# Attention's weighted values summed by accumulating DMAs in DRAM, and two more unused matmuls in the head

## The chip, the core and the metric

The kernel runs on one core of one Trainium2 chip. The metric is the device time of one execution in microseconds (us). The engines are TensorE (PE, matmul; PEld is its weight load), VectorE (DVE), ScalarE (ACT), GpSimd (POOL) and SyncE (SP, which here only issues DMAs).

## The reference

The input x is 2048 x 640, float32. It is normalised; a local dilated attention and a gated bilinear network work on the normalised rows, and the result joins both:

```python
xn = _layernorm(x)
qkv = xn @ wqkv                       # 32 heads of 20
idx = pos[:, None] - (arange(8) * 2)  # 8 places, every second row back
logits = einsum("bhsd,bhswd->bhsw", q, k[idx]) * scale   # masked where idx < 0
o = einsum("bhsw,bhswd->bhsd", softmax(logits), v[idx])
s = o @ wo
h = (xn @ w_gate) * (xn @ w_up)       # 640 -> 1536
g = silu(h @ w_down)
return x + s * g
```

## The kernel before

The 2048 rows lie as 16 tiles of 128; a tile holds rows a fixed distance apart, so that the eight places of a row's window lie in the same partition or in the one before it. Matmuls run on high and low halves of each float32 operand in three passes (`mm3`, line 87: high x high, one low, the other low), which a split on ScalarE (line 79, high) and a subtraction, mostly on GpSimd (line 80, low), prepare.

The program is written in one order, engine by engine, and each engine works through its own queue in that order. Its stages:

1. Head: loads, three unused products of the identity (line 147), normalisation and transposes, the first qkv and the first gate and up matmuls.
2. Attention stage, about 110 to 550 us. The heads lie in six groups (5, 5, 5, 5, 6, 6), each group in two halves of eight tiles: twelve units. `unit(u)` computes q, k and v of a unit (`qkv`, 8 x 15 matmuls); between units stand three or four pieces of `gate_up`, each for one f of 12 (128 columns of the network) and one of four chunks of 512 rows: 15 matmuls for the gate (PSUM tile g), 15 for up (u). Their product h goes to DRAM (`h_scr`).
3. The attention of a unit is a generator, `attention(u)`. `advance(budget)` steps it between the matmuls: each yield names about its own VectorE time, and the budget is about the matmuls' time. So the order in which VectorE's work is written follows the credit. Of the eight places two are done at a time (`PAIRS`): four products of q and k with their sums, the softmax, then four products of weights and values (line 279), three additions of pairs (line 287), one of the pair's halves (line 290), and a store into `o_scr` by SP (line 292).
4. The last f (f1): behind its piece 1 the attention is drained, the output weights wo are split (two of five behind each of the first two pieces, one behind the third), and tile 0 of o is loaded. Before its piece 3 stand the load of wd, the transposes of tile 0, and the loads of tiles 1 to 7 of o (`load_o`, line 384).
5. Output projection (16 tiles), then the product with w_down (in seven products for each pair of tiles), gating and the output.

SP issues all DMAs and does it in order: a DMA that waits for an engine holds those behind it. A finished piece multiplies u and g on VectorE while a generator runs (line 333), and with ScalarE and GpSimd otherwise (lines 335, 336).

Tiles with one tag share buffers in rotation: `t` (x tiles, attention's products, o tiles, h tiles) has two.

Of the kernel before, what the change touches and what calls it, by code (L numbers as in the profile page):

```python
# [11 lines left out]
F32 = mybir.dt.float32  # L12
F32R = mybir.dt.float32r
AF = mybir.ActivationFunctionType
ALU = mybir.AluOpType
# [16 lines left out]
GROUPS = [5, 5, 5, 5, 6, 6]  # L32
GOFF = [sum(GROUPS[:g]) * DH for g in range(len(GROUPS))]
# [4 lines left out]
PAIRS = range(0, W, 2)  # L38
# [9 lines left out]
def kernel(  # L48
# [9 lines left out]
    nc = tc.nc  # L58
# [5 lines left out]
    dr = ctx.enter_context(tc.tile_pool(name="dr", bufs=1, space=DRAM))  # L64
# [12 lines left out]
    def split(eng, raw, hi, lo):  # L77

        nc.scalar.activation(hi, raw, AF.Copy)  # L79
        eng.tensor_sub(lo, raw, hi.bitcast(F32))  # L80
# [20 lines left out]
    def split_wq(g, eng, ks=(0, KD)):  # L101
        c3 = 3 * GROUPS[g] * DH
        if g not in wq:
            wq[g] = st([P, KD, c3], "wqh", 1, F32R), st([P, KD, c3], "wql", 1, F32R)
        for k0, k1, t in wq_raw[g]:
            if ks[0] <= k0 < ks[1]:
                split(eng, t, wq[g][0][:, k0:k1], wq[g][1][:, k0:k1])

    wf_raw, wf = {}, {}
# [18 lines left out]
        for i in range(n):  # L128
            xt[s + i] = t[:, i, :]

    xa, xb = st([P, 3, D], "t", 2), st([P, 3, D], "t", 2)
    load_x(0, 1, xa[:, 0:1], (0, HALF, D))
    load_x(1, 1, xa[:, 1:2])
    load_wq(0, ((0, 1, 2, 3), (3, 4, 5)))
# [8 lines left out]
    load_x(15, 1, xb[:, 2:3])  # L143
    ident = st([P, P], "ident", 1)
    make_identity(nc, ident)
    for _ in range(3):
        nc.tensor.matmul(pt([P, 3, P], "q", 4), ident, ident.unsqueeze(1).to_broadcast([P, 3, P]), start=True,
                         stop=True)
    eps_t = st([P, 1], "eps", 1)
    nc.vector.memset(eps_t, EPS)  # L150

    o_scr = [dr.tile([2, P, NE, GROUPS[g] * DH], F32, name=f"o_scr{g}") for g in range(len(GROUPS))]
    h_scr = dr.tile([NT, P, KF, P], F32, name="h_scr")
    s_scr = dr.tile([NT, P, D], F32, name="s_scr")

# [43 lines left out]
    def trans(s):  # L199
        transposed(xt[s], *xT_tile(s))  # L200
# [34 lines left out]
    def attention(u):  # L235
        g, r = UN[u]
        nh = GROUPS[g]
        c = nh * DH
        q, kv = q_t[u], kv_t[u]
        pair, one, small = [(n + 155) / 950 for n in (2 * NE * c, NE * c, NE * nh * W)]  # L240
        lg = st([P, NE * nh, W], "lg", 2)
        e = st([P, NE * nh, W], "e", 1)
        yield 1.0

        def places(a, j):

            y = kv[:, a, j:j + NE, :].rearrange("p i c -> p (i c)")
            return bass.AP(y.tensor, y.offset, [y.ap[0], [c, 2], y.ap[1]])

        def pair_tile():  # L250
            return st([P, 2, NE * c], "t", 2)

        def heads(y):
            return y.rearrange("p a (n d) -> p a n d", d=DH)

        for j in PAIRS:
            t = pair_tile()
            nc.vector.tensor_mul(t, q.rearrange("p i c -> p (i c)").unsqueeze(1).to_broadcast([P, 2, NE * c]),  # L258
                                 places(0, j))
            yield pair  # L260
            nc.vector.tensor_reduce(out=lg[:, :, j:j + 2].rearrange("p n a -> p a n"), in_=heads(t),  # L261
                                    op=ALU.add, axis=AX.X)
            yield pair
        m0 = lg[0:1].rearrange("p (i h) w -> p i h w", h=nh)
        nc.vector.tensor_add(m0, m0, mask.unsqueeze(2).to_broadcast([1, NE, nh, W]))
        sm = st([P, 2, NE * nh], "sm", 2)
        nc.vector.tensor_reduce(out=sm[:, 0, :], in_=lg, op=ALU.max, axis=AX.X)
        nc.vector.tensor_sub(lg, lg, sm[:, 0, :].unsqueeze(2).to_broadcast([P, NE * nh, W]))
        yield 3 * small
        nc.scalar.activation(e, lg, AF.Exp, scale=SCALE)  # L270
        yield small
        nc.vector.tensor_reduce(out=sm[:, 0, :], in_=e, op=ALU.add, axis=AX.X)
        nc.vector.reciprocal(sm[:, 1, :], sm[:, 0, :])
        nc.vector.tensor_mul(e, e, sm[:, 1, :].unsqueeze(2).to_broadcast([P, NE * nh, W]))
        yield 3 * small

        def weighted(j, t):
            pw = e[:, :, j:j + 2].rearrange("p n a -> p a n").unsqueeze(3).to_broadcast([P, 2, NE * nh, DH])
            nc.vector.tensor_mul(heads(t), pw, heads(places(1, j)))  # L279

        acc, t = pair_tile(), pair_tile()
        weighted(PAIRS[0], acc)
        yield pair
        for j in PAIRS[1:]:
            weighted(j, t)
            yield pair
            nc.vector.tensor_add(acc, acc, t)  # L287
            yield pair
        o = st([P, NE, c], "o", 1)
        nc.vector.tensor_add(o.rearrange("p i c -> p (i c)"), acc[:, 0, :], acc[:, 1, :])  # L290
        yield one
        nc.sync.dma_start(o_scr[g][r], o)

    running = []

    def advance(budget):
        credit[0] += budget
        while running and credit[0] > 0:
            try:
                credit[0] -= next(running[0][1])  # L300
            except StopIteration:
                running.pop(0)
        if not running:
            credit[0] = 0
# [75 lines left out]
    def load_o(s, n, t):  # L380

        for g in range(len(GROUPS)):
            c = GROUPS[g] * DH
            nc.sync.dma_start(t[:, :, GOFF[g]:GOFF[g] + c], o_scr[g][s // NE, :, s % NE:s % NE + n, :])
        for i in range(n):
            o_t[s + i] = t[:, i]

    def trans_o(s):
        if s == NT - 2:
            oT[s] = st([P, KD, P], "hs", 2, F32R), st([P, KD, P], "hs", 2, F32R)  # L390
        else:
            tag, n = ("kv", 2) if s == 0 else ("wf", 4) if s < NT - 2 else ("t", 2)
            y = st([P, 2, KD, P], tag, n, F32R)
            oT[s] = y[:, 0], y[:, 1]
        transposed(o_t.pop(s), *oT[s])
# [55 lines left out]
    def load_h(n):  # L451

        a, b = 2 * n, 2 * n + 1
        if n % 2:
            ta, tb = st([P, KF, P], "t", 2), st([P, KF, P], "t", 2)
            nc.sync.dma_start(ta, h_scr[a])
            nc.sync.dma_start(tb, h_scr[b])
            h_raw[n] = {"A11": ta[:, :KH], "A12": ta[:, KH:], "A21": tb[:, :KH], "A22": tb[:, KH:]}
        else:
            h_raw[n] = {}  # L460
            for name, s, k, tag, m in (("A11", a, 0, "wraw", 3), ("A21", b, 0, "wraw", 3),
                                       ("A22", b, KH, "wraw", 3), ("A12", a, KH, "o", 1)):
                h_raw[n][name] = st([P, KH, P], tag, m)
                nc.sync.dma_start(h_raw[n][name], h_scr[s][:, k:k + KH])
# [92 lines left out]
    mv1 = moments(1, 1)  # L557
    split_wq(0, nc.gpsimd, (0, 3))
    trans(0)
    split_wq(0, nc.gpsimd, (3, KD))  # L560
    load_x(13, 1, xa[:, 0:1])
    norm(1, 1, mv1)
# [88 lines left out]
    for ch in range(NCH):  # L651
        gate_up(f0, ch)
        if ch == 0:
# [3 lines left out]
            t = load_wo((4,))  # L657
    for ch in range(NCH):
        if ch == 3:
            load_wd(0)  # L660
            trans_o(0)
            load_o(1, 1, st([P, 1, D], "hs", 2))
            load_o(2, 3, st([P, 3, D], "t", 2))
            load_o(5, 3, st([P, 3, D], "t", 2))
        gate_up(f1, ch)
        if ch < 3:
            for k in ((0, 1), (2, 3), (4,))[ch]:
                split_wo(k)
        if ch == 1:
            drain(len(UN) - 2)  # L670
            load_o(0, 1, t[:, 1:2])
        if ch == 2:
            advance(1e9)

    load_wd(1)
    o_next = {3: (8, 3), 6: (11, 3), 9: (14, 2)}
    n_prod = 7 * NT // 2
    for s in range(NT):
        k, part = divmod(s - 1, 2)
        if s == 1:  # L680
            begin_wd()
        if s + 1 < NT:
            trans_o(s + 1)
        if s in o_next:
            load_o(*o_next[s], st([P, o_next[s][1], D], "t", 2))
# [12 lines left out]
    load_sx(0)  # L698
    load_sx(1)
    load_h(1)  # L700
    AHEAD = 4
    sum_h(1)
# [4 lines left out]
    for m in range(n_prod):  # L707
        n, j = divmod(m, 7)
# [52 lines left out]
```

## Time and profile before

| | |
|---|---|
| median of 3 runs | 804.54 us (803.0 to 804.66) |
| profiled execution | 803.25 us, span 801.5 us |
| granted TensorE clock, mean | 0.998 |
| PE busy | 791.7 us |
| VectorE busy | 635.2 us |
| ScalarE busy | 236.7 us |
| GpSimd busy | 137.7 us |
| moved by DMA | 90.07 MB, 34.7% of 16 engines' span on SP's queue |

The span runs from the first to the last instruction; some 1.8 us of the execution's time lie around it. Busy times overlap between engines. The chain of the page follows the work that ended last back to the start: what stands there sets the time, what does not is hidden. A row of a timeline or of the groups gives, after the arrow in brackets, what ended the idle time before it.

### The profile page before, as it was taken

How to read it: one execution, taken by the hardware profiler on the slowest of the kernel's cores; microseconds unless marked ns; L12 is line 12 of the kernel's file. 1: busy time of each engine (PE TensorE's matmuls, PEld its weight loads, DVE VectorE, ACT ScalarE, POOL GpSimd, SP SyncE). 2: the span in 40 equal slices, each digit the busy share in tenths (PEclk: the TensorE clock that was granted, in tenths of full speed). 3: DMA queues.
4: the chain of work that ended last, by engine and by line, in shares of the span. 5: the costliest groups of instructions: out<-in, count | busy, mean ns of one | idle time of the engine just before them, and what ended most of it. 6: DMA issues, size and time to landing. Idle time of an engine off the chain costs nothing.

```text
span 801.5 us, 11434 instructions
## 1 busy us (share of the span) xinstructions
PE 791.7 (99%) x4564; PEld 721.5 (90%) x4564; DVE 635.2 (79%) x638; ACT 236.7 (30%) x560; POOL 137.7 (17%) x109
## 2 busy tenths in 40 slices
PE   8999999999999999999999999999999999999997
PEld 6889898898898898898989889888899999999997
DVE  7676899999999979997999999990144457878775
ACT  4323212121112111211121112102355554444442
POOL 5201210122012100500231001104266500000000
PEclk9999999999999999999999999999999999999999
DMA  9122012141122221313141222422867464565523
GB/s 318 63 80 89 28 61 79 51 121 48 49 88 86 87 70 60 116 39 97 49 137 42 68 72 78 129 61 75 214 191 206 139 251 136 201 224 185 178 99 132
DMA packets 68413, 90.07 MB, mean 112 GB/s; under 512 B 16952, under 2 KB 48776, under 8 KB 68360
## 3 DMA queue, kind: packets, MB, share of 16 engines
q1 hardware_dynamic: 68360, 89.34, 34.7%
q8 instruction: 36, 0.59, 0.3%
q14 instruction: 17, 0.14, 0.1%
HBM read 51.90 MB, written 28.31 MB: 100 GB/s over the span
## 4 chain that ended last, share of the span: by engine, by line
PE 96%; DMA 1%; POOL 1%; issue 1%; ACT 0%; DVE 0%; SPq 0%; POOLq 0%
PE q L87 35%; PE g L87 20%; PE u L87 20%; PE q L526 10%; PE u L526 5%; PE g L526 3%; PE q L195 2%; DMA wraw<-in_wqkv 1%; DMA hs<-o_scr 0%; POOL wf L80 0%; POOL wql L80 0%; ACT xc L196 0%; DVE q L512 0%; POOL hs L336 0%; SPq L127 0%
## 5 line engine op out<-in xcount | busy, mean ns | idle before, releaser
L87 PE MATMUL g<-xc,wf 128*128 128x512 f32 (+1 forms) x735 | 176.3, 391 | 0.1
L87 PE MATMUL u<-xc,wf 128*128 128x512 f32 (+1 forms) x735 | 176.1, 390 | 0.0
L87 PEld LDWEIGHTS u<-xc,wf 128*128 128x128 f32 x735 | 135.6, 187 | 32.2
L87 PE MATMUL q<-wqh,xc 128*128 128x300 f32 (+1 forms) x960 | 161.8, 311 | 2.1 <-ACT xc L196 1.6
L87 PEld LDWEIGHTS g<-xc,wf 128*128 128x128 f32 x735 | 135.2, 188 | 31.2 <-POOL wf L80 0.3
L87 PEld LDWEIGHTS q<-wqh,xc 128*128 128x128 f32 x960 | 146.8, 189 | 4.2 <-ACT xc L196 2.1
L258 DVE TENSOR_TENSOR t<-q,kv 128x1600 f32<-128x1600 f32 (+1 forms) x48 | 101.7, 2119 | 9.1 <-DMA kv<-kv 9.1
L279 DVE TENSOR_TENSOR t<-e,kv 128x1600 f32<-128x1600 f32 (+1 forms) x48 | 97.6, 2053 | 1.1
L261 DVE TENSOR_REDUCE lg<-t 128x80 f32<-128x1600 f32 (+1 forms) x48 | 92.6, 1930 | 1.2
L322 ACT ACTIVATE gs<-g 128x512 f32<-128x512 f32 x48 | 28.8, 599 | 207.5 <-PE g L87 198.8
L80 POOL TENSOR_TENSOR wf<-wraw,wf 128x256 fp32r<-128x256 f32 (+2 forms) x22 | 44.8, 2053 | 249.1 <-ACT wf L79 249.1
L87 PE MATMUL q<-wql,xc 128*128 128x300 f32 (+1 forms) x480 | 87.0, 311 | 0.2 <-POOL wql L80 0.2
L287 DVE TENSOR_TENSOR t<-t,t 128x1600 f32<-128x1600 f32 (+1 forms) x36 | 78.0, 2166 | 1.1
L226 ACT ACTIVATE kv<-q 128x200 f32<-128x200 f32 (+1 forms) x96 | 33.4, 348 | 145.9 <-PE q L87 145.9
L87 PEld LDWEIGHTS q<-wql,xc 128*128 128x128 f32 x480 | 74.8, 189 | 0.6 <-POOL wql L80 0.5
L526 PE MATMUL q<-xc,wf 128*128 128x320 f32 x432 | 67.3, 309 | 0.0
L526 PEld LDWEIGHTS q<-xc,wf 128*128 128x128 f32 x432 | 64.3, 188 | 0.0
L80 POOL TENSOR_TENSOR wql<-wraw,wqh 128x300 fp32r<-128x300 f32 (+4 forms) x15 | 33.4, 2254 | 147.8 <-ACT wqh L79 147.8
L197 DVE TENSOR_TENSOR wf<-q,wf 128x512 fp32r<-128x512 f32 (+1 forms) x26 | 11.5, 486 | 41.7 <-ACT wf L196 41.7
L87 PE MATMUL q<-wf,wf 128*128 128x320 f32 x156 | 36.8, 317 | 0.0
L197 DVE TENSOR_TENSOR xc<-q,xc 128x512 fp32r<-128x512 f32 (+1 forms) x32 | 13.9, 484 | 20.7 <-ACT xc L196 20.7
L333 DVE TENSOR_TENSOR hs<-u,gs 128x512 f32<-128x512 f32 x39 | 26.6, 683 | 0.8 <-issue 0.8
(144 smaller groups left out, 900.9 us busy)
## 6 DMA issues: line engine op xcount, KB each, us to landing
h_scr<-hs SPq DMA_DIRECT2D x48, 256.0 KB, 2.3
wraw<-in_wgu SPq DMA_DIRECT2D x12, 640.0 KB, 4.5
t<-h_scr SPq DMA_DIRECT2D x8, 768.0 KB, 7.4
s_scr<-gs SPq DMA_DIRECT2D x16, 320.0 KB, 2.3
hs<-s_scr SPq DMA_DIRECT2D x16, 320.0 KB, 3.7
gs<-in_x SPq DMA_DIRECT2D x16, 320.0 KB, 4.2
out<-q SPq DMA_DIRECT2D x15, 320.0 KB, 2.4
wraw<-h_scr SPq DMA_DIRECT2D x12, 384.0 KB, 6.1
```

Of the source, the lines that this page charges most:

```text
L80: eng.tensor_sub(lo, raw, hi.bitcast(F32))
L87: nc.tensor.matmul(acc, a, b, start=first and n == 0, stop=last and n == len(runs) - 1)
L195: nc.tensor.transpose(p[:, k - k0, :], src[:, k * P:(k + 1) * P], ident)
L197: nc.vector.tensor_sub(lo[:, k0:k1, :], p, hi[:, k0:k1, :].bitcast(F32))
L226: nc.scalar.activation(kv_t[u][:, :, W - 1 + i, :], p[:, c:].rearrange("p (a c) -> p a c", a=2), AF.Copy)
L258: nc.vector.tensor_mul(t, q.rearrange("p i c -> p (i c)").unsqueeze(1).to_broadcast([P, 2, NE * c]), places(0, j))
L261: nc.vector.tensor_reduce(out=lg[:, :, j:j + 2].rearrange("p n a -> p a n"), in_=heads(t), op=ALU.add, axis=AX.X)
L279: nc.vector.tensor_mul(heads(t), pw, heads(places(1, j)))
L287: nc.vector.tensor_add(acc, acc, t)
L322: nc.scalar.activation(gs, pp[0], AF.Copy)
L333: nc.vector.tensor_mul(hs, pp[1], gs)
L526: nc.tensor.matmul(p, y[:, i, k], wd_t[name][k][:, l], start=new and r == 0, stop=r == len(runs) - 1, skip_group_check=True)
```

## The change

- The additions of attention's products (lines 287, 290) go. Each of a unit's four products gets a tile of its own. SP stores the first two into two accumulators in DRAM, `o_scr[g][r][0]` and `[1]`; GpSimd issues the third and fourth as DMAs that add to them.
- Two more accumulating DMAs on GpSimd's queue finish a unit: the second accumulator is added to the first, then the first's second half to its first half. `merge()` issues one of them; they wait in a list. It is called in the next unit's generator, behind the third pair of the logits and ahead of the weighted values, and in loops behind pieces 1 and 2 of the last f, which empty the list.
- The yields for the removed additions go too, so a generator ends with less credit.
- `t` has four buffers instead of two, and the program reserves 2048 bytes for GpSimd's DMA descriptors.
- The head has four unused products at its start instead of three, and one between the first transposes and the second part of the first weight split.

```diff
-    for _ in range(3):
+    for _ in range(4):
+        idle_product()
...
-    o_scr = [dr.tile([2, P, NE, GROUPS[g] * DH], F32, name=f"o_scr{g}") for g in range(len(GROUPS))]
+    o_scr = [[[dr.tile([P, 2, NE * n * DH], F32, name=f"o_scr{g}_{r}{a}") for a in range(2)] for r in range(DIL)]
+             for g, n in enumerate(GROUPS)]
...
             yield pair
+            if j == PAIRS[2]:
+                merge()
...
-        acc, t = pair_tile(), pair_tile()
-        weighted(PAIRS[0], acc)
-        yield pair
-        for j in PAIRS[1:]:
+        merge()
+        for n, j in enumerate(PAIRS):
+            t = pair_tile()
             weighted(j, t)
             yield pair
-            nc.vector.tensor_add(acc, acc, t)
-            yield pair
-        o = st([P, NE, c], "o", 1)
-        nc.vector.tensor_add(o.rearrange("p i c -> p (i c)"), acc[:, 0, :], acc[:, 1, :])
-        yield one
-        nc.sync.dma_start(o_scr[g][r], o)
+            if n < 2:
+                nc.sync.dma_start(o_scr[g][r][n], t)
+            else:
+                nc.gpsimd.dma_start(o_scr[g][r][n % 2], t, accum_op=ALU.add)
+        a, b = o_scr[g][r]
+        merges.append((a, b))
+        merges.append((a[:, 0], a[:, 1]))
+
+    merges = []
+
+    def merge():
+
+        if merges:
+            y, z = merges.pop(0)
+            nc.gpsimd.dma_start(y, z, accum_op=ALU.add, max_dma_last_dim=3200)
...
     trans(0)
+    idle_product()
     split_wq(0, nc.gpsimd, (3, KD))
...
         if ch == 1:
             drain(len(UN) - 2)
+            while merges:
+                merge()
             load_o(0, 1, t[:, 1:2])
         if ch == 2:
             advance(1e9)
+            while merges:
+                merge()
...
-    nc = bacc.Bacc("TRN2", target_bir_lowering=False, num_devices=1)
+    nc = bacc.Bacc("TRN2", target_bir_lowering=False, num_devices=1, dynamic_dma_scratch_size=2048)
```

More of the change, by code (lines that the diff above doesn't have):

```diff
@@ L129, in load_x @@
             xt[s + i] = t[:, i, :]
-    xa, xb = st([P, 3, D], "t", 2), st([P, 3, D], "t", 2)
+    xa, xb = st([P, 3, D], "t", 4), st([P, 3, D], "t", 4)
     load_x(0, 1, xa[:, 0:1], (0, HALF, D))
@@ L145, with idle_product @@
     make_identity(nc, ident)
-    for _ in range(3):
+    def idle_product():
         nc.tensor.matmul(pt([P, 3, P], "q", 4), ident, ident.unsqueeze(1).to_broadcast([P, 3, P]), start=True,
                          stop=True)
+    for _ in range(4):
+        idle_product()
     eps_t = st([P, 1], "eps", 1)
     nc.vector.memset(eps_t, EPS)
-    o_scr = [dr.tile([2, P, NE, GROUPS[g] * DH], F32, name=f"o_scr{g}") for g in range(len(GROUPS))]
+    o_scr = [[[dr.tile([P, 2, NE * n * DH], F32, name=f"o_scr{g}_{r}{a}") for a in range(2)] for r in range(DIL)]
+             for g, n in enumerate(GROUPS)]
     h_scr = dr.tile([NT, P, KF, P], F32, name="h_scr")
@@ L239, in attention @@
         q, kv = q_t[u], kv_t[u]
-        pair, one, small = [(n + 155) / 950 for n in (2 * NE * c, NE * c, NE * nh * W)]
+        pair, small = [(n + 155) / 950 for n in (2 * NE * c, NE * nh * W)]
         lg = st([P, NE * nh, W], "lg", 2)
@@ L250, in pair_tile @@
         def pair_tile():
-            return st([P, 2, NE * c], "t", 2)
+            return st([P, 2, NE * c], "t", 4)
         def heads(y):
@@ L383, in load_o @@
             c = GROUPS[g] * DH
-            nc.sync.dma_start(t[:, :, GOFF[g]:GOFF[g] + c], o_scr[g][s // NE, :, s % NE:s % NE + n, :])
+            nc.sync.dma_start(t[:, :, GOFF[g]:GOFF[g] + c], o_scr[g][s // NE][0][:, 0].rearrange("p (i c) -> p i c", c=c)[:, s % NE:s % NE + n])
         for i in range(n):
@@ L391, in trans_o @@
         else:
-            tag, n = ("kv", 2) if s == 0 else ("wf", 4) if s < NT - 2 else ("t", 2)
+            tag, n = ("kv", 2) if s == 0 else ("wf", 4) if s < NT - 2 else ("t", 4)
             y = st([P, 2, KD, P], tag, n, F32R)
@@ L454, in load_h @@
         if n % 2:
-            ta, tb = st([P, KF, P], "t", 2), st([P, KF, P], "t", 2)
+            ta, tb = st([P, KF, P], "t", 4), st([P, KF, P], "t", 4)
             nc.sync.dma_start(ta, h_scr[a])
@@ L662 @@
             load_o(1, 1, st([P, 1, D], "hs", 2))
-            load_o(2, 3, st([P, 3, D], "t", 2))
-            load_o(5, 3, st([P, 3, D], "t", 2))
+            load_o(2, 3, st([P, 3, D], "t", 4))
+            load_o(5, 3, st([P, 3, D], "t", 4))
         gate_up(f1, ch)
@@ L684 @@
         if s in o_next:
-            load_o(*o_next[s], st([P, o_next[s][1], D], "t", 2))
+            load_o(*o_next[s], st([P, o_next[s][1], D], "t", 4))
         if 0 <= k < KH:
```

## The prediction

> **What bounds the kernel now.** I read the busy shares and the chain of the page first, then the table of busy time by stage (PE busy and its instructions, then PEld, DVE, ACT, POOL, then granted clock, DMA share, GB/s).
>
> ```profile
> PE 791.7 (99%) x4564; PEld 721.5 (90%) x4564; DVE 635.2 (79%) x638; ACT 236.7 (30%) x560; POOL 137.7 (17%) x109
> ...
> PE 96%; DMA 1%; POOL 1%; issue 1%; ACT 0%; DVE 0%; SPq 0%; POOLq 0%
> ```
>
> ```profile
> 0.00:16.00 16.00, 12.14 (x47) 8.62 (x48) 10.68 (x34) 7.42 (x20) 7.66 (x15) 0.89 0.87 295
> ...
> 110.00:350.00 240.00, 240.00 (x1327) 212.29 (x1326) 228.82 (x164) 47.16 (x133) 35.92 (x12) 1.00 0.25 76
> 350.00:512.00 162.00, 162.00 (x835) 145.61 (x834) 153.56 (x100) 30.89 (x85) 17.73 (x6) 1.00 0.25 76
> ...
> 555.00:575.00 20.00, 19.64 (x101) 16.37 (x101) 1.77 (x4) 6.33 (x14) 8.47 (x6) 1.00 0.64 155
> ...
> 795.00:801.50 6.50, 1.66 (x12) 1.40 (x10) 3.44 (x6) 0.49 (x2) 0.00 (x0) 0.97 0.28 102
> ```
>
> TensorE is the bound. Through the whole attention stage (110 to 512 us) PE is busy 402 of 402 us at full clock. VectorE is nearly full there too (228.82 of 240), but nothing on PE waits for it. PE is idle in three places only: the head, the last 6 us, and 0.36 us near 569, the one place where something behind the head is late for PE. Work taken off VectorE can therefore save nothing by itself; what counts is where the new GpSimd (POOL) waits meet PE.
>
> **Part 1, VectorE's adds go.** Line 287 is gone, and so is line 290.
>
> ```profile
> L287 DVE TENSOR_TENSOR t<-t,t 128x1600 f32<-128x1600 f32 x24 | 52.1, 2170 | 0.7
> ...
> L287 DVE TENSOR_TENSOR t<-t,t 128x1920 f32<-128x1920 f32 x12 | 25.9, 2157 | 0.4
> ...
> L290 DVE TENSOR_TENSOR o<-t 128x800 f32<-128x800 f32 x8 | 10.1, 1262 | 0.2
> ...
> L290 DVE TENSOR_TENSOR o<-t 128x960 f32<-128x960 f32 x4 | 6.9, 1720 | 0.1
> ```
>
> 52.1 + 25.9 + 10.1 + 6.9 = 95.0 us of VectorE work, 7.9 per unit. Its worth is 0: PE had no idle time in that stage. It only makes ScalarE's wait for the logits and the attention's end earlier; both had room.
>
> **Part 2, the accumulating transfers in the middle.** Per unit, SP issues two stores instead of one, and POOL issues two accumulating stores, one merge of the two accumulators, and one merge of its two halves: 48 DMAs on POOL. Each waits: the accumulates for SP's store and VectorE's product, the first merge for both accumulates, the second merge for the first. Queued behind them on POOL are the splits of the weights (line 80), on which PE waits for the low parts.
>
> ```profile
> 290.73 3.50 PE g L87 x15
> ```
>
> ```profile
> L80 POOL TENSOR_TENSOR wf<-wraw,wf 128x1280 fp32r<-128x1280 f32 x10 | 34.2, 3419 | 246.5 <-ACT wf L79 246.5
> ...
> L79 ACT ACTIVATE wf<-wraw 128x1280 fp32r<-128x1280 f32 x10 | 12.7, 1268 | 1.7 <-PE u L87 1.7
> ```
>
> A split of the next f is issued between the two halves of piece 1 and needed after that piece's second half (the 3.50 of a row like this) and pieces 2 and 3 (four more halves, 14.0), its low part after 10 of 15 matmuls more (2.3): 19.8 us. The split itself is 1.27 + 3.42, so 15.1 us of cover remain; the splits of wqkv have at least as much, three or four pieces. The second merge is emitted some 8 us behind the first, since the generator's credit runs at about VectorE's pace. A merge that lands in under some 20 us therefore costs nothing in the middle. Taken: 0.
>
> SP's 12 further stores take 0.33 us each to issue, like the 12 it had; loads queued behind them wait for VectorE, which now is ahead of its old times.
>
> **Part 3, the last merges.** Unit 11's two merges are issued only in the loop behind piece 1 of the last f, so on POOL they stand behind the split of wo 2 and 3 and before piece 2's product (line 336) and the split of wo 4. Chain and timeline of that place:
>
> ```profile
> 558.09 1.55 POOL wql L80
> 559.64 2.63 issue
> ...
> 562.28 1.30 POOL hs L336
> ...
> 563.60 0.37 SPq L337
> ...
> 564.07 0.45 SPq L426
> ...
> 565.07 0.46 SPq L384
> ...
> 565.57 3.78 DMA hs<-o_scr
> ```
>
> ```profile
> 562.28 1.30 POOL L336 TENSOR_TENSOR hs<-hs,gs 128x512 f32<-128x512 f32 x1 [2.64 <-issue]
> ...
> 569.49 1.01 PE L195 MATMUL q<-ident,hs 128*128 128x128 f32 x5 [0.36 <-DMA hs<-o_scr]
> ```
>
> Read it as a relay: POOL's product of piece 2 (562.28) lets SP store it (563.60); behind that store SP has the loads of wd and then the loads of o's tile 1 (565.07 on); these land, and PE transposes tile 1 at 569.49, having waited 0.36 us already. There is no slack in this relay, so whatever delays POOL's product at 562.28 delays PE one for one. POOL has 2.64 us free before it. Into that gap now go: the issue of merge 1, its landing (merge 2 waits for it), the issue of merge 2.
>
> Merge 1 adds 128 x 1920 floats, 960 KB, from DRAM to DRAM. The trace has no accumulating DMA; the nearest rows:
>
> ```profile
> wraw<-in_wgu SPq DMA_DIRECT2D x12, 640.0 KB, 4.5
> t<-h_scr SPq DMA_DIRECT2D x8, 768.0 KB, 7.4
> ...
> L384 SPq DMA_DIRECT2D hs<-o_scr x6: 430/430/460, 565.1 to 567.5; - x6
> ...
> DMA to landing us min/median/max: 2.0/3.2/5.0
> ```
>
> ```profile
> 16.00:17.00 1.00, 1.00 (x11) 1.00 (x10) 0.97 (x2) 0.91 (x4) 1.00 (x2) 1.00 1.04 417
> 559.00:561.00 2.00, 2.00 (x10) 1.61 (x9) 0.00 (x0) 0.00 (x0) 0.64 (x1) 1.00 0.60 127
> 561.00:563.00 2.00, 2.00 (x13) 1.60 (x12) 0.00 (x0) 1.45 (x3) 0.72 (x1) 1.00 0.03 7
> ```
>
> Lower end: 983,040 bytes at the best rate, 417 GB/s (2.4 us), on top of the shortest landing, 2.0: 4.4 us. Upper end: destination and source are both read, so twice the 768 KB row: 14.8. I take 7.4, the row nearest in size; the DMA engines are nearly empty there (0.03 at 561 to 563). An issue on POOL lies between SP's 0.43 and POOL's own longest instruction of that kind, 3.42; I take 1.0, nearer to the first, since both write descriptors for about as many rows. The delay is 1.0 + 7.4 + 1.0 - 2.64 = **6.8 us**; ends 0.43 + 4.4 + 0.43 - 2.64 = 2.6 and 3.42 + 14.8 + 3.42 - 2.64 = 19.0.
>
> The Trainium skill, "DMA: Bandwidth & Descriptors", in the section on the anatomy of one DMA on the SWDGE path, fits a GpSimd DMA as 2.0 us plus its bytes over 436,000 per us. An estimate from it is 4.3 us for merge 1, with which the delay would be 3.7 instead of 6.8; no run here shows an accumulating transfer yet.
>
> A stall of 7 us also lets the clock fall. The head shows the price:
>
> ```profile
> 7.00:8.00 1.00, 0.04 (x1) 0.00 (x0) 0.23 (x2) 0.89 (x3) 1.00 (x2) 1.00 1.03 391
> ...
> 9.00:10.00 1.00, 1.00 (x6) 0.94 (x5) 0.84 (x4) 0.08 (x1) 1.00 (x2) 0.62 1.04 394
> 10.00:11.00 1.00, 0.84 (x4) 0.51 (x4) 0.90 (x4) 0.00 (x0) 1.00 (x2) 0.50 0.87 215
> 11.00:12.00 1.00, 1.00 (x6) 1.00 (x5) 1.00 (x2) 0.00 (x0) 0.71 (x1) 0.50 0.88 307
> 12.00:13.00 1.00, 1.00 (x7) 0.85 (x6) 0.97 (x4) 0.48 (x2) 0.00 (x0) 0.67 0.99 374
> ```
>
> After a stretch with little PE work the granted clock is 0.62, 0.50, 0.50, 0.67 for four us: 0.38 + 0.50 + 0.50 + 0.33 = 1.7 us lost. I add 1.7 behind the stall (bounds 0 and 1.7). Together **+8.5 us**.
>
> **Part 4, the head.** One more unused product stands before the first transposes, one between them and the first qkv.
>
> ```profile
> 1.37 4.21 PE L147 MATMUL q<-ident 128*128 128x384 f32 x6 [1.37 <-POOL ident masks.py:199]
> 6.28 0.76 PE L195 MATMUL q<-ident,t 128*128 128x128 f32 x5 [0.70 <-DVE t L188]
> 8.10 1.26 PE L87 MATMUL q<-wqh,xc 128*128 128x300 f32 x5 [1.06 <-ACT xc L196]
> ...
> 10.57 0.62 PE L87 MATMUL q<-wql,xc 128*128 128x300 f32 x1 [0.16 <-POOL wql L80]
> ...
> 12.23 0.92 PE L195 MATMUL q<-ident,t 128*128 128x128 f32 x5
> ```
>
> One product is 4.21 / 3 = 1.4 us. They fill the idle 0.70 and 1.06 and overrun each by up to 0.7; the second overrun is covered, because that qkv then waits for POOL's split at 10.57 anyway. Filled gaps may keep the clock up from 9 to 13, worth 1.7 at most; on the path I see about the 0.16 by which the second transposes were slower (0.92 against 0.76) and as much before them. Taken: **-0.3 us**, bounds -1.7 and +0.7.
>
> **Sum.** 6.8 + 1.7 - 0.3 = +8.2 us. The profiled execution took 803.25 us (span 801.5), so 811.5; the median of the runs shown is 1.3 above it, 804.54, so I predict **812.7 us**.
>
> **The rivals.** A change within 0.2%, 1.6 us, is about what a measurement of this kernel can tell from none.
>
> - *Forecast, slow merges*: delay of 5 to 10 us plus the clock, +6.4 to +11.4. Chance 0.47.
> - *Quick merge*: it lands in about 4.4 us, by the lower rows, with issues of 1.0; delay 3.8 and too short for the clock to fall: +3.5, 808.0 us. For it: the DMA engines are empty there. Against: two streams are read and one written, all in DRAM. Chance 0.22. The fit named above falls on this case. The Trainium skill, "TensorE: Matmul & The Clock Gate", Part 1, lets the clock fall after about one idle window of 3.4 us, by which this case would pay the 1.7 as well; no stall of that length stands alone in this trace.
> - *Both ends high*: merge 1 near 14.8, or POOL held while each DMA drains: delay 12 to 19, 817 to 825 us. Chance 0.11.
> - *The middle stalls too*: merges above 20 us, so that POOL's splits are late past their 15.1 us of cover, at each of about ten f: 5 us each would be 850 us. For it: DMA share 0.25 in the middle, and 50 MB more to move (eight units with 4,000 KB more each, four with 4,800). Against: 76 GB/s there against 417 in the head. Chance 0.03.
> - *No change*: the wait hides because merge and issues together take under about 4 us, that is, 2.64 and the measurement's 1.6: 804.5 us. Chance 0.11.
> - *Faster*: the same hidden wait, and the head's two products hold the clock from 9 to 13 with the whole 1.7 on the path: 802.8 us. It decides only if the delay is under 0.1 us. For it: the clock rows; against it: POOL's split and VectorE, not PE, end the waits in the head. Chance 0.06.
>
> Slower 0.47 + 0.22 + 0.11 + 0.03 = 0.83, same 0.11, faster 0.06. The delay's lower end of 2.6 without a clock fall and with the head's best, -1.7, gives 805.4; the range begins at 804.6, to hold about half of no change, and goes to 823, which holds most of the high case. It leaves out the faster case, the middle, the other half of no change and the tail of the high one.
>
> **What would show it.** In the profile after: PE without idle time from 30 to 569 us, as before; VectorE near 540 us busy; at 569 PE idle 4 to 12 us ahead of the transposes of tile 1, released by the DMA into hs, with the granted clock falling behind it; POOL's product of piece 2 some 7 us later than 562.28. It is wrong if PE at 569 waits as little as before (then merges are cheap), if PE waits for POOL's splits between 110 and 512, or if the head ends more than 1 us earlier or later.

## The result and the profile after

| | before | changed |
|---|---|---|
| median | 803.92 us (803.0 to 804.66, 4 runs) | 835.98 us (830.24 to 837.83, 4 runs) |
| ratio | | 1.039, 95% interval 1.033 to 1.044 |
| profiled execution | 803.25 us, span 801.5 | 835.15 us, span 833.4 |

The changed kernel is slower by 32 us; 812.7 was predicted, in a range that ended at 823. A few executions fell into a slower state with a lower granted clock: ratios are of the others alone, medians and ranges hold all (one of four in last_merges_later and shifts_on_scalar, one of nine in zero_additions), and the profiled execution of shifts_on_scalar was itself such a one, so only its landing times and the order of its instructions are read.

Busy shares, DMA queues (packets, MB, share of 16 engines) and shares of the chain, from the page of the changed kernel:

```profile
PE 800.0 (96%) x4568; PEld 725.2 (87%) x4568; DVE 532.9 (64%) x587; ACT 238.2 (29%) x563; POOL 176.7 (21%) x160
...
q1 hardware_dynamic: 70088, 105.07, 38.0%
q0 software_dynamic: 9216, 36.70, 24.9%
...
PE 72%; DMA 10%; DVE 8%; issue 4%; SPq 2%; POOL 2%; ACT 1%; DVEq 0%; POOLq 0%; ACTq 0%
```

VectorE lost about the work that was foreseen (635.2 to 532.9), but the chain, which was 96% PE, now goes through DMA and VectorE for 18%. By stage (same columns as before):

```profile
110.00:350.00 240.00, 235.51 (x1304) 207.78 (x1303) 158.29 (x125) 47.44 (x133) 53.01 (x37) 1.00 0.75 180
350.00:512.00 162.00, 153.45 (x785) 137.92 (x784) 114.50 (x83) 28.21 (x82) 27.34 (x21) 0.98 0.71 175
...
560.00:580.00 20.00, 18.38 (x79) 14.52 (x78) 0.00 (x0) 6.37 (x11) 11.58 (x9) 1.00 0.58 130
580.00:600.00 20.00, 11.69 (x52) 8.77 (x51) 0.89 (x2) 3.19 (x6) 7.88 (x7) 0.85 0.80 170
600.00:620.00 20.00, 20.00 (x129) 19.98 (x128) 5.88 (x13) 8.42 (x22) 5.14 (x7) 0.89 0.67 187
```

The DMA share went from 0.25 to over 0.7. PE, full from 110 to 512 before, is idle there for 4.49 + 8.55 = 13.0 us, and for 8.3 in the stretch 580 to 600. What ended PE's idle time (total, times, longest), with VectorE's largest wait for a DMA behind it:

```profile
PE u L87 <- DVE hs L348: 13.7, 6, 5.0
PE q L200 <- DMA hs<-o_scr: 7.7, 1, 7.7
...
DVE t L263 <- DMA kv<-kv: 113.3, 8, 17.9
```

The same wait of VectorE in the kernel before:

```profile
DVE t L258 <- DMA kv<-kv: 9.1, 3, 4.1
```

The second row is the relay of the prediction. The first and third were not in it: the shifts of k and v (line 236 of the changed kernel), DMAs that copy a tile's last places one partition on and that the first logits of a unit need, land late. Their time from issue to landing, after and then before:

```profile
DMA to landing us min/median/max: 2.5/7.9/15.0
```

```profile
DMA to landing us min/median/max: 2.4/3.0/5.4
```

How that reaches PE is seen at unit 5, in the timelines of the changed kernel (SP, POOL, VectorE, PE), and then in two rows of its windows (the last columns: clock, DMA share, GB/s):

```profile
244.22 0.50 SPq L294 DMA_DIRECT2D o_scr<-t  x1
...
246.59 3.27 SPq L236 DMA_DIRECT2D kv<-kv  x4
...
246.03 0.90 POOL L296 DMA_DIRECT2D o_scr<-t  x1 [13.24 <-DVE t L286]
249.58 0.86 POOL L296 DMA_DIRECT2D o_scr<-t  x1 [2.65 <-DMA o_scr<-t]
...
243.70 3.55 DVE L286 TENSOR_TENSOR t<-e,kv 128x1600 f32<-128x1600 f32 x2
261.87 1.83 DVE L263 TENSOR_TENSOR t<-q,kv 128x1600 f32<-128x1600 f32 x1 [14.63 <-DMA kv<-kv]
...
267.20 0.68 DVE L348 TENSOR_TENSOR hs<-u,gs 128x512 f32<-128x512 f32 x1
...
267.94 3.76 PE L87 MATMUL u<-xc,wf 128*128 128x512 f32 x15 [3.39 <-DVE hs L348]
```

```profile
251.00:253.00 2.00, 2.00 (x11) 1.59 (x10) 0.00 (x0) 1.60 (x3) 1.50 (x1) 1.00 0.94 198
...
255.00:257.00 2.00, 2.00 (x10) 1.59 (x10) 0.00 (x0) 0.00 (x0) 0.10 (x1) 1.00 1.00 226
```

VectorE, freed of the additions, has done unit 4's last two products by 247.25. So the unit's second store (SP 244.22) and both accumulating transfers (POOL 246.03, 249.58) are issued within 5 us of unit 5's shifts (246.59); the 16 DMA engines are full (0.94 and 1.00 in the two rows), and VectorE has the shifts it needs only at 261.87. VectorE has nothing else left and waits 14.63 us at the front of its queue. The product hs of u and g, written three operations behind, comes at 267.20; it reads the PSUM tile that the next u needs, and PE waits 3.39 us. The kernel before at the same place:

```profile
241.43 6.79 SPq L231 DMA_DIRECT2D kv<-kv  x4
...
259.34 0.33 SPq L292 DMA_DIRECT2D o_scr<-o  x1
...
256.46 1.82 DVE L287 TENSOR_TENSOR t<-t,t 128x1600 f32<-128x1600 f32 x1
259.23 1.82 DVE L258 TENSOR_TENSOR t<-q,kv 128x1600 f32<-128x1600 f32 x1
```

There the additions keep VectorE busy until 259, the unit's single store goes out 18 us behind the first shifts, and the first logits find them landed. At unit 10's pieces the changed kernel's wait is long enough for the clock to fall:

```profile
482.36 6.44 PE L87 MATMUL u<-xc,wf 128*128 128x512 f32 x15 [4.99 <-DVE hs L348]
```

Such a row takes 3.76 us at full clock, so the stall costs 4.99 + 2.68.

### The profile page after: what moved, and what is told of

Its sections match the earlier page's. It is cut to its first block, busy times and chain, and to the rows that moved or that the text cites. A ratio compares the mean times of both kernels' runs of the same rounds, so it can differ in the third digit from the quotient of the medians.

```text
span 833.4 us, 11514 instructions
## 1 busy us (share of the span) xinstructions
PE 800.0 (96%) x4568; PEld 725.2 (87%) x4568; DVE 532.9 (64%) x587; ACT 238.2 (29%) x563; POOL 176.7 (21%) x160
## 3 DMA queue, kind: packets, MB, share of 16 engines
q0 software_dynamic: 9216, 36.70, 24.9%
## 4 chain that ended last, share of the span: by engine, by line
PE 72%; DMA 10%; DVE 8%; issue 4%; SPq 2%; POOL 2%; ACT 1%; DVEq 0%; POOLq 0%; ACTq 0%
PE q L87 32%; PE u L87 12%; PE q L541 10%; PE g L87 9%; DMA kv<-kv 7%; PE u L541 5%; DVE t L263 4%; PE g L541 3%; PE q L200 2%; DMA o_scr<-t 1%; DVE lg L266 1%; DVE hs L348 1%; DVE t L286 1%; DMA h_scr<-hs 1%; DMA wraw<-in_wqkv 0%
## 5 line engine op out<-in xcount | busy, mean ns | idle before, releaser
L87 PE MATMUL u<-xc,wf 128*128 128x512 f32 (+1 forms) x735 | 179.7, 396 | 15.5 <-DVE hs L348 13.7
L263 DVE TENSOR_TENSOR t<-q,kv 128x1600 f32<-128x1600 f32 (+1 forms) x48 | 97.8, 2038 | 128.3 <-DMA kv<-kv 113.3
L286 DVE TENSOR_TENSOR t<-e,kv 128x1600 f32<-128x1600 f32 (+1 forms) x48 | 95.1, 2031 | 0.3
L296 POOL DMA_DIRECT2D o_scr<-t x24 | 21.4, 893 | 172.8 <-DVE t L286 82.5
L307 POOL DMA_DIRECT2D o_scr<-o_scr x24 | 22.5, 938 | 131.0 <-DMA o_scr<-o_scr 78.2
L80 POOL TENSOR_TENSOR wql<-wraw,wqh 128x300 fp32r<-128x300 f32 (+4 forms) x15 | 25.6, 1752 | 33.1 <-ACT wqh L79 33.1
## 6 DMA issues: line engine op xcount, KB each, us to landing
o_scr<-t POOLq DMA_DIRECT2D x16, 800.0 KB, 10.2
```

Source lines behind the costliest of these rows:

```text
L87: nc.tensor.matmul(acc, a, b, start=first and n == 0, stop=last and n == len(runs) - 1)
L296: nc.gpsimd.dma_start(o_scr[g][r][n % 2], t, accum_op=ALU.add)
L307: nc.gpsimd.dma_start(y, z, accum_op=ALU.add, max_dma_last_dim=3200)
```

## The experiments

The two losses each have their theories. *Relay*: the last merges delay tile 1's transposes, as predicted. *Meeting*: the accumulating traffic falls on the shifts. *Order*: the credit and the shorter work of VectorE put the wait for the shifts at the front of its queue. A rival to the last two is that GpSimd's transfers cost by themselves, wherever they stand. The diffs show the lines that matter; dots stand for the rest.

**last_merges_later**: the two `while merges` loops behind pieces 1 and 2 go; one stands behind the last piece.

```diff
-            while merges:
-                merge()
...
+    while merges:
+        merge()
     load_wd(1)
```

> The two merges of the last unit are issued behind the last f instead of behind its piece 1; all else as in the changed kernel (835.98 us). Relay theory (prediction, part 3): GpSimd's product of piece 2 no longer stands behind the merges' 7.6 us landing, the 7.7 us wait of TensorE at the transposes of tile 1 goes, and the slow clock behind it: 10 to 11 us less, about 825 us. Rival (the wait is only handed on): the merges then hold the splits of wd or the load of tile 8, and TensorE waits there as long: 833 to 836 us. The middle stage is untouched in both.

823.13 us (818.19 to 831.97), ratio 1.022 (1.017 to 1.028): by the ratios about 13 us less, give or take 6, and PE no longer waits for tile 1. VectorE's wait for the shifts stays (117.4 us). Not all of the 13 need be the relay's: the profiled execution also lost less in the middle, which the edit does not touch (PE idle from 110 to 512 for 6.9 us instead of 13.0), so the middle's loss seems to vary between executions.

**thin_transfers**: GpSimd's DMAs move one eighth of their columns (the rest of the sums is left out).

```diff
-                nc.gpsimd.dma_start(o_scr[g][r][n % 2], t, accum_op=ALU.add)
+                nc.gpsimd.dma_start(o_scr[g][r][n % 2][:, :, :c], t[:, :, :c], accum_op=ALU.add)
...
-        merges.append((a, b))
-        merges.append((a[:, 0], a[:, 1]))
+        merges.append((a[:, :, :c], b[:, :, :c]))
+        merges.append((a[:, 0, :c], a[:, 1, :c]))
```

> Every DMA on GpSimd's queue keeps its place, its waits and its issue, but moves only the first 100 or 120 columns of each row (an eighth of the bytes), so o is not the full sum. Contention theory (the accumulating transfers occupy the DMA engines, the shifts of k and v land in 7 to 15 us instead of 3, VectorE waits for them with the gate and up products behind it, and TensorE then lacks a free PSUM buffer): shifts land in 3 to 4 us, VectorE waits for them under 40 us in total, and the time falls to 806 to 812 us, the rest being the last merges. Order theory (the generators end earlier, so SP and VectorE reach the shifts at a bad moment whatever the traffic): VectorE still waits over 80 us in total and the time stays above 822 us.

804.95 us, ratio 1.002 (1.001 to 1.003). As many DMAs and waits, few bytes, and both losses nearly go; the shifts land in a median of 3.5 us. VectorE's wait for the shifts missed my number, 88.6 us instead of under 40: an early VectorE waits at every unit, and this costs PE nothing as long as the shifts land in time.

**plain_copies**: the same DMAs copy instead of adding (the output holds unsummed products).

```diff
-                nc.gpsimd.dma_start(o_scr[g][r][n % 2], t, accum_op=ALU.add)
+                nc.gpsimd.dma_start(o_scr[g][r][n % 2], t)
...
-            nc.gpsimd.dma_start(y, z, accum_op=ALU.add, max_dma_last_dim=3200)
+            nc.gpsimd.dma_start(y, z, max_dma_last_dim=3200)
```

> GpSimd's DMAs copy instead of adding: same bytes moved, same places and waits, but the destination isn't read (o is not the sum). If the adding itself is what fills the DMA engines (24.9% of their span for 36.7 MB, against 38.0% for 105 MB on SP's queue, 1.9 times as much per byte): GpSimd's stores land in 4 to 6 us instead of 10, the shifts in 4 to 6, and 812 to 820 us. If it is the bytes alone, or that two queues share the engines: shifts still 7 us and more, 828 to 836 us.

809.07 us, ratio 1.007 (1.005 to 1.008), below both expectations. Its queue line and its middle:

```profile
q0 software_dynamic: 6400, 36.70, 12.6%
...
110.00:350.00 240.00, 240.00 (x1329) 212.47 (x1328) 178.37 (x133) 48.35 (x134) 46.22 (x39) 1.00 0.54 182
350.00:512.00 162.00, 162.00 (x834) 145.63 (x833) 119.20 (x82) 30.86 (x85) 23.99 (x22) 1.00 0.54 190
```

The same 36.70 MB take 12.6% of the engines' time instead of 24.9%. Stores on GpSimd's queue land in 6.3 us instead of 10.2, the merges of 960 KB in 5.0 instead of 8.4, the shifts in 4.4. With the order as written in the changed kernel and an early VectorE (84.6 us of waits for the shifts), PE is full from 110 to 512. So the adding, not the moving, is the larger part of the traffic's price. The copies also went in fewer packets, 6,400 instead of 9,216; how much of the price that is was not taken apart.

**old_credit**: the yields of the removed additions are put back, without the additions.

```diff
             yield pair
+            if n:
+                yield pair
+            if n == 3:
+                yield (NE * c + 155) / 950
```

> The yields that went with the additions are put back without the additions, so the work of VectorE stands at the same places among the matmuls as before the change; all transfers as in the changed kernel. Order theory: the four products spread over the old time, the next unit's first logits come later and find k and v landed; VectorE's waits for the shifts fall under 40 us and the time to 812 to 818 us (the last merges stay). Contention theory: the transfers move with the products and collide again; waits stay above 80 us in total, 828 us or more.

814.08 us, ratio 1.014 (1.011 to 1.017): 21.9 less, with every accumulating transfer in place. The time is the one that the order theory expected; VectorE's wait for the shifts, 80.7 us instead of under 40, is not, so neither theory alone holds. PE's waits for hs go from 13.7 to 3.5 us, the shifts' landing to a median of 5.3; the wait at tile 1 stays, 8.6.

**later_and_old_credit**: the two repairs together.

> The two repairs together: unit 11's merges are issued behind the pieces of the last f (alone: 823.13 us, 12.9 below the changed kernel) and the yields of the removed additions are put back without the additions (alone: 814.08 us, 21.9 below it). Accumulating transfers, their number and bytes stay. If the two losses are separate (one at the relay to tile 1's transposes, one in the middle from the order in VectorE's queue), the gains add: 835.98 - 12.9 - 21.9 = 801.2, bounded below by the kernel before, 803 to 804, because PE has no idle time left to save; I expect 803 to 806, with the wait of PE for tile 1 under 2 us and its waits for VectorE's product of u and g at most those of the second run (3.5 us in all). If old credit had only shortened the last attention's lateness, which the later merges shorten as well, the gains overlap and the time stays above 808.

808.45 us (805.54 to 809.77), ratio 1.006 (1.004 to 1.007), above the 803 to 806 expected. The gains do not quite add. In the middle PE still loses 2.24 us, and a new wait at the output's first tiles (below) remains (the row is the middle's):

```profile
110.00:470.00 360.00, 357.76 (x1933) 317.69 (x1932) 252.78 (x192) 69.72 (x196) 72.44 (x54) 1.00 0.74 181
```

**head_only**: the kernel before with the two further unused products.

```diff
-    for _ in range(3):
+    for _ in range(4):
+        idle_product()
...
     trans(0)
+    idle_product()
```

> The kernel before with nothing but the two further unused products in the head. My prediction's step: -0.3 us, bounds -1.7 to +0.7. From the trace after, where the second qkv of the head starts at 21.79 us as before: 0.0. Both lie within the 0.2% that can be told from no change: 802.7 to 803.7 us beside a kernel before at 803.2. Above 805 or below 801.5 both would be wrong, and part of the changed kernel's loss or gain would come from the head.

803.24 us, ratio 0.9996 (0.9987 to 1.0005): no difference that can be told.

**logits_later**: last_merges_later with another first yield of a unit's attention.

```diff
-        yield 1.0
+        yield 8.0
```

> As last_merges_later (823.13 us), and one number more: the first yield of a unit's attention is 8.0 instead of 1.0, so the first four logits' products, which wait for the shifts of k and v, are written some 7 us later into VectorE's queue, behind more of the gate and up products on which PE waits. The transfers, their bytes and their number stay as they are. If the loss in the middle comes from where VectorE's wait for the shifts stands in its queue, the late landing is covered: 804 to 808 us, and PE's waits for VectorE's product of u and g go from 8.3 us to under 2. If it comes from the traffic itself, wherever the wait stands: about 823.

807.23 us (804.63 to 810.54), ratio 1.004 (1.003 to 1.006): by the ratios about 15 us from one number. Its middle, and VectorE's wait:

```profile
110.00:470.00 360.00, 360.00 (x1945) 320.33 (x1944) 270.40 (x198) 71.19 (x197) 76.68 (x56) 1.00 0.78 191
```

```profile
DVE t L263 <- DMA kv<-kv: 8.0, 4, 3.3
```

PE is full at a DMA share of 0.78: the traffic alone does not stall it. But the number moved more than the wait: the products, and with them the accumulating transfers, came later too (unit 5: shifts at 239.81, accumulating transfers at 254.78), and the shifts land in a median of 3.9 us. So this run does not tell order from meeting, as I had meant it to.

**shifts_on_scalar**: last_merges_later with line 236 on ScalarE's queue.

```diff
-                    nc.sync.dma_start(kv_t[u][p0 + 1:p1 + 1, :, i0 - 1:i1 - 1, :],
+                    nc.scalar.dma_start(kv_t[u][p0 + 1:p1 + 1, :, i0 - 1:i1 - 1, :],
```

> As last_merges_later (823.13 us), but the shifts of k and v are issued on ScalarE's queue instead of SP's. In the changed kernel the shifts stand on SP behind the stores of two products of the unit before, which wait for VectorE; GpSimd's accumulating transfers share the DMA engines with the shifts whatever queue those are issued from. If SP's queue makes the shifts late, their time from issue to landing falls from a median of 7.9 us towards the 3.0 of the kernel before and the time to 808 to 815. If the sharing of the DMA engines makes them late: landing stays at 6 to 8 us and the time at 820 to 826.

830.96 us, ratio 1.032 (1.028 to 1.036), above the 820 to 826 expected. Landing stays at 7.1 us (7.6 with SP), so the queue of issue does not by itself make it late. It is no clean test of SP's own delay: on ScalarE the shifts stood behind an exponential that waits for VectorE, and unit 5's went out at 246.66. The Trainium skill, "DMA: Bandwidth & Descriptors", section on issuing engines, says that DMAs of all of them run on the same 16 engines and interleave; these landing times agree.

**wait_later_only**: as logits_later, with the 7.0 given back over the first three weighted products.

```diff
-            yield pair
+            yield pair if n == 3 else pair - 7 / 3
```

> As logits_later (first yield 8.0), but the 7.0 of credit are given back over the first three weighted products (each yields pair - 7/3), so that a unit's last product, its stores and its accumulating transfers stand about where they stood in last_merges_later, on top of the next unit's shifts; only the first logits are later. logits_later moved both (in its trace unit 5's shifts were issued at 239.8 us and the accumulating transfers at 254.8; in last_merges_later 245.9 and 246.1). If the place of VectorE's wait is what matters: 805 to 809 us, with the shifts' landing still at a median of 6 to 8 us. If it is the meeting of the transfers: landing 6 to 8 us and the time at 815 to 823.

806.06 us, ratio 1.003 (1.002 to 1.004). Unit 5, SP, POOL and VectorE:

```profile
244.36 2.06 SPq L294 DMA_DIRECT2D o_scr<-t  x2
246.51 4.42 SPq L236 DMA_DIRECT2D kv<-kv  x4
...
249.84 0.90 POOL L296 DMA_DIRECT2D o_scr<-t  x1 [10.50 <-DVE t L286]
251.91 0.86 POOL L296 DMA_DIRECT2D o_scr<-t  x1 [1.16 <-DMA o_scr<-t]
...
253.07 0.69 DVE L348 TENSOR_TENSOR hs<-u,gs 128x512 f32<-128x512 f32 x1 [3.53 <-issue]
254.86 3.21 DVE L263 TENSOR_TENSOR t<-q,kv 128x1600 f32<-128x1600 f32 x1 [1.10 <-DMA kv<-kv]
```

At this unit stores, shifts and accumulating transfers go out nearly as close together as in the changed kernel (the accumulating ones 2 to 4 us later), but hs now stands ahead of the logits that wait. PE has no idle time from 110 to 560. The meeting is milder too: VectorE has the shifts at 254.86 instead of 261.87, their median, 4.9, is below the 6 to 8 that I expected (the longest is 13.1), and VectorE's wait for them is 23.5 us in all instead of 117.4. So another written order is enough, with all the traffic in place; how much of it is the place of the wait and how much the milder meeting, this run does not tell either.

**no_additions**: the kernel before without the additions, only half of the first product stored.

```diff
-            nc.vector.tensor_add(acc, acc, t)
-            yield pair
-        o = st([P, NE, c], "o", 1)
-        nc.vector.tensor_add(o.rearrange("p i c -> p (i c)"), acc[:, 0, :], acc[:, 1, :])
-        yield one
-        nc.sync.dma_start(o_scr[g][r], o)
+        nc.sync.dma_start(o_scr[g][r], acc[:, 0, :].rearrange("p (i c) -> p i c", c=c))
```

> The kernel before with the change's first part alone: the additions of VectorE's products and their yields go, and only the first product's first half is stored, as one store by SP as before (the other products are left out of the output); t has four buffers, no accumulating transfer. My prediction's step, that VectorE's freed time is worth 0: 803 to 804 us. Being early is harmless without transfers to meet, if the loss is the transfers'; if an emptied queue of VectorE costs by itself, since the wait for the shifts then stands at its front, the landing of about 3.0 us stays and the time rises to 806 or more, with waits of PE for VectorE's product of u and g.

803.49 us, ratio 0.9994 (0.9985 to 1.0003). VectorE at unit 5:

```profile
249.14 3.06 DVE L258 TENSOR_TENSOR t<-q,kv 128x1600 f32<-128x1600 f32 x1 [8.67 <-DMA kv<-kv]
```

The early VectorE waits at the front of its queue here too (90.4 us in all), but the shifts are there at 249.14 instead of 261.87, and PE notices nothing.

**zero_additions**: later_and_old_credit, with VectorE's additions really done, of a zero.

```diff
+    zero = st([P, 1], "zero", 1)
+    nc.vector.memset(zero, 0.0)
...
             if n:
+                nc.vector.tensor_add(t, t, zero.unsqueeze(1).to_broadcast([P, 2, NE * c]))
                 yield pair
             if n == 3:
+                nc.vector.tensor_add(t[:, 0, :], t[:, 0, :], zero.to_broadcast([P, NE * c]))
                 yield (NE * c + 155) / 950
```

> later_and_old_credit (808.45 us) with VectorE's additions really done again: each of the second to fourth products has a zero added in place, and half of the fourth once more, so VectorE works about as long as in the kernel before, at the old places, while all accumulating transfers stay. If the loss comes from VectorE being early (stores and accumulating transfers of a unit meet the shifts of the next, and the wait for these stands at the front of VectorE's queue), the old load puts it back: 803.5 to 806 us, and VectorE's wait for the shifts goes from 75 us to under 20. If the transfers cost by themselves, VectorE's load does not matter or makes it worse: 808 to 812.

802.71 us (799.3 to 812.75), ratio 0.999 (0.997 to 1.001). VectorE's wait for the shifts fell to 14.9 us, as expected. The time says nothing by itself, because the gate and up matmuls took 390 ns instead of 395. The new tile had moved all tiles behind it. Two runs took this apart.

**before_and_tile**: the kernel before and that tile, unused.

> The kernel before with one more tile of 4 bytes for each partition behind the tile of epsilon (as in zero_additions), set to zero once by VectorE and used by nothing. It moves all tiles behind it, the split weights wf among them, by 32 bytes: wf begins at a multiple of 64 bytes instead of 32 beyond one. In zero_additions, the only run so far with that tile, the 1410 matmuls of the gate and up took a mean of 390 ns instead of 395 in all the others, 168.1 + 167.9 us instead of 172.2 + 172.2. If that comes from the place of the tiles: 803.9 - 8.4 = 795.5 us (794 to 797), with 390 ns. If it comes from something else in zero_additions (VectorE's work, the transfers): 803 to 804.5.

797.73 us (796.86 to 797.87), ratio 0.993 (0.991 to 0.994): faster than both kernels, and just above the 794 to 797 expected. Its two groups of the 128x512 matmuls (busy, mean ns, idle before):

```profile
L87 PE MATMUL g<-xc,wf 128*128 128x512 f32 x705 | 168.1, 390 | 0.0
L87 PE MATMUL u<-xc,wf 128*128 128x512 f32 x705 | 167.9, 390 | 1.1 <-DVE hs L335 1.1
```

In the kernel before:

```profile
L87 PE MATMUL g<-xc,wf 128*128 128x512 f32 x705 | 172.2, 395 | 0.0
```

The matmuls give 8.4 us; 5.7 arrive. PE is idle 2.2 us more (796.0 - 784.0 against 801.5 - 791.7), 1.1 of it for VectorE's hs: with PE faster, VectorE begins to matter.

**small_additions**: zero_additions without the tile; VectorE adds the tile of epsilon (1e-5) that was there.

> zero_additions without the new tile: what VectorE adds to the products is the tile of epsilon (1e-5), already there, so all tiles lie where they lay in later_and_old_credit (808.45 us). Only VectorE's 36 and 12 additions differ from that run. If VectorE being early is what makes the middle lose: PE's waits for VectorE's product of u and g (1.6 us there) and the first logits' wait for the shifts (75 us there) are gone, and the time falls to 804.5 to 807. If the transfers cost by themselves: 808 to 812, as zero_additions would be with its 8.4 us of faster matmuls taken off (802.7 + 8.4 = 811).

805.61 us (804.32 to 811.18), ratio 1.004 (1.002 to 1.006). The middle, VectorE's wait and the stretch 580 to 600:

```profile
110.00:470.00 360.00, 359.92 (x1944) 320.22 (x1943) 336.54 (x233) 70.32 (x197) 82.29 (x56) 1.00 0.77 186
...
580.00:600.00 20.00, 17.47 (x113) 17.21 (x112) 8.72 (x12) 8.19 (x23) 9.90 (x11) 0.91 0.91 250
```

```profile
DVE t L264 <- DMA kv<-kv: 15.9, 5, 6.0
```

With VectorE nearly as busy as before (336.54 us; 342.11 in the same stretch of the kernel before), the accumulating transfers cost PE 0.08 us in 360, though the shifts still need a median of 5.7 us. So the rival, a price of the transfers wherever they stand, is out for the middle. By its time it is not told apart from later_and_old_credit (the intervals overlap); the middle's rows tell it: 359.92 us of PE work there against 357.76. What is left lies at 580 to 600, where the late merges share the DMA engines with the loads of o: PE waits 2.53 us for ScalarE's copy, and the clock falls. I did not follow that further.

## Why the prediction was wrong

**The step that failed is Part 2's "Taken: 0"** for the accumulating transfers in the middle: in the changed kernel's trace PE is idle there (110 to 512 us) for 13.0 us, nearly all of it for VectorE's product hs behind the wait for shifts that land in a median of 7.9 us instead of 3.0, and it loses 2.7 more at the low clock behind unit 10's wait. Part 2 rested on "loads queued behind them wait for VectorE, which now is ahead of its old times"; I took being early as harmless. Part 1 (worth 0) and Part 2 are each right alone and wrong together: no_additions shows the early VectorE alone at 803.49, small_additions the transfers under the old load with a middle 0.08 us from full. Together they cost about 15 us, give or take 4, by the ratios of last_merges_later (1.022) and of the two orders that leave PE full in the middle (1.004 and 1.003). I had looked at who waits on POOL, the splits, and asked whether merges come back within 20 us; they did (medians of 7.2 us for 800 KB and 8.4 for 960 KB), and PE waited 0.6 us in all for a split. I did not ask what else lies on the DMA engines when the transfers start, nor what stands behind the wait for the shifts on VectorE. The row that would have told it, the 9.1 us of waits for the shifts with a longest of 4.1, was small only because the additions kept VectorE late; their removal was the change.

**The rival "the middle stalls too"** had the stage right, with a chance of 0.03, and the wrong cause, POOL's splits.

**Part 3, the last merges**, holds, by place and nearly by size. Timelines of POOL and PE, and then a window:

```profile
581.74 0.91 POOL L307 DMA_DIRECT2D o_scr<-o_scr  x1
590.21 1.19 POOL L307 DMA_DIRECT2D o_scr<-o_scr  x1 [7.56 <-DMA o_scr<-o_scr]
590.95 1.75 POOL L351 TENSOR_TENSOR hs<-hs,gs 128x512 f32<-128x512 f32 x1
...
599.02 1.30 PE L200 MATMUL q<-ident,hs 128*128 128x128 f32 x5 [7.67 <-DMA hs<-o_scr]
```

```profile
600.00:602.00 2.00, 2.00 (x10) 2.00 (x9) 0.89 (x2) 0.77 (x2) 0.00 (x0) 0.50 1.01 225
```

An issue takes 0.91 us (1.0 taken), the second merge waits 7.56 for the first (7.4 taken), and PE waits 7.67 where it had waited 0.36: 7.3 against 6.8. The clock stays at 0.50 for some 5 us of PE's work and costs about 2.6 where I took 1.7. By place that makes 7.3 + 2.6 = 9.9 us, where 8.5 were predicted; with the merges moved about 13 went, and the spread of that run holds the difference. That 7.4 met the landing so closely is partly luck: it was the row of a plain load of 768 KB, and plain copies of the merges' own 960 KB landed in 5.0. An estimate of 4.3 us for that merge by the fit of the Trainium skill, "DMA: Bandwidth & Descriptors", was low by half against the median of 8.4 in the trace; the plain copies of 960 KB, 5.0, are near it. The case of quick merges is out. Its premise that a delay of 3.8 us is too short for the clock to fall does not hold either: a wait of 3.67 us (last_merges_later, at 267.54) brought it to 0.50.

**Part 4, the head**: -0.3 taken; head_only shows nothing, within 0.7 us either way, which does not tell 0 from -0.3.

**The sum** by the trace: idle time of PE from 110 to 512, 13.0; the clock behind unit 10's wait, 2.7; at the attention of unit 11, which ends the stage, 3.0; the relay, 8.3 - 0.4 and 2.6 of clock: 29 of 31.9. The 3.0 are these two waits of PE:

```profile
548.91 3.77 PE L87 MATMUL u<-xc,wf 128*128 128x512 f32 x15 [1.39 <-DVE hs L348]
...
571.79 3.76 PE L87 MATMUL u<-xc,wf 128*128 128x512 f32 x15 [1.62 <-ACT hs L350]
```

The first hs stands on VectorE behind two products (541.38 to 548.26). Ahead of the second, the store of a product lands 11.63 us after its issue, and POOL's accumulating transfer, which waits for it, holds the next hs.

## What to carry to other kernels

Work taken off an engine that is not the bound moves everything behind it forward, its DMAs too: ask what those now meet, and which wait comes to the front of that engine's queue. Where two edits are each free alone, cost them together: the first may be the cover of the second. And a wait in a queue costs by what stands behind it: writing the waiting operation later, with urgent ones ahead of it, was worth about 15 us here without a byte less traffic, though the transfers moved a little with it.

## What the runs showed of the hardware

- A DMA on GpSimd's queue that adds to its destination took twice the engines' time of a copy: 24.9% of a span of 833.4 us against 12.6% of 807.1 for the same 36.70 MB (a factor of 2.0), and its stores of 800 KB landed in a median of 10.2 us against 6.3, or 4.1 for plain stores of that size by SP.
- In the changed kernel a wait of PE of 3.39 us left the granted clock at full; waits of 4.99 and 7.67 brought it to 0.50 for 5 to 6 us of work. The length alone does not decide: waits of 2.95 us (old_credit, at 471.53) and 2.53 us (small_additions, at 588.66) brought it to 0.50 too, for some 3.3 us, beginning 0.2 to 1.4 us after PE had work again. The Trainium skill, "TensorE: Matmul & The Clock Gate", Part 1, has it fall after about one idle window of 3.4 us; the first three waits agree with that, the two short ones do not.
- A shift of tiles by 32 bytes brought the mean of 1410 matmuls from 395 to 390 ns (8.4 us of busy time) and made the kernel before 5.7 us faster. The split weights wf begin 32 bytes behind a multiple of 64 in both kernels and at such a multiple with the tile. Other tiles moved as well, so which placement does it is not shown.
